# A strided convolution with its gradients on one core: 258-wide leaf planes, one transfer to turn both row parities, rows stored by parity

## The chip, the cores and the metric

The kernel runs on one core of a Trainium2 chip. The metric is device time in microseconds (us), from launch to end. Each number of the trace comes from one profiled execution; the time that counts is the median of several runs. The engines are TensorE (PE: matmuls; PEld: its weight loads), VectorE (DVE), ScalarE (ACT), GpSimd (POOL) and SyncE (SP). SP computes nothing here: it issues DMAs, one after the other, and a DMA that has to wait for its data holds back all that stand behind it in SP's queue.

## The reference

The forward pass is a convolution along time of 31 taps and stride 2, a normalisation of each channel over time, and a GELU. The outputs are the forward result and the gradients of all four inputs.

```python
B, T, D, K = 2, 16000, 256, 31          # x: (2, 16000, 256), w: (31, 256, 256), bf16
L = (T - K) // 2 + 1                    # 7985
h = sum over i of einsum('blc,cd->bld', x[:, i:i + 2 * L:2, :], w[i])
mu, var = mean and variance of h over l, for each image and channel
h = (h - mu) / sqrt(var + 1e-5) * gn_gamma + gn_beta
out = gelu(h, tanh form)
out_0 = out;  out_1 .. out_4 = vjp(grad_out): dx, dw, dgamma, dbeta
```

## The kernel before

The three convolutions (forward, gradient of x, gradient of w) are computed by a fast-FIR scheme with three branches A, B, C on each of several levels, so that fewer matmuls are needed and the operands are sums and differences of rows. The program has five stages. F0 and F1 are the forward pass of image 0 and image 1; beside F1, the element-wise work of image 0 (`gelu_unit`, 8 units) is done. G0 and G1 are the gradient of x (`input_grad`), in 8 chunks (4 of each image) of 2 halves and 3 branches; beside the first chunks the 8 gelu units of image 1 run. W is the gradient of w (`weight_grad`), in 9 combinations.

In G, a chunk's error rows are loaded with `e_load` (two DMAs, `dyd` and `hd`, for each half of the channels), made ready by `e_comp` (line 1201, 1203 or 1208, 1210, 1212, 1221) and spread into planes with channels on the partitions: a plane holds 256 rows and 2 or so from the chunk before, once for the even and once for the odd rows (index `j`). `g_sums` makes the sums of planes (line 1272). Matmuls (line 1317) read them as weights. `g_three_b` copies a PSUM bank with ACT (line 1344), `g_seed` combines banks with DVE (line 1384), `g_evac` takes results out of PSUM with ACT (`keep`, line 826) into `HO`, a single buffer, which a DMA stores to `out_1`; ACT writes it again only when that store has landed.

W needs the same planes with rows on the partitions. So `dl_turn` turns them by DMA: for each chunk nine leaves (3 branches by 3), each into one of four tiles `DNO`, and stores the tile to DRAM (`dl_d`). A leaf takes four turns, for two halves of the channels and two parities of the row, of 128 partitions by 256 columns (65,536 bytes) each, and one store of 262,144 bytes, in which the even and the odd row of a pair lie together in 1,024 bytes. That makes 8 x 9 x 4 = 288 turns and 72 stores. `d_tile` loads 19 rows a partition of one leaf in W. In F1, `gelu_unit` of image 0 turns its output by the same helper, in pieces of 128 partitions by 1,024 columns (262,144 bytes), two a unit.

Within a gelu unit of image 1, ACT's sigmoid (line 1098) writes the tile that the unit before has stored to `dyd`: it waits until that store has landed.

All DMAs of more than 4,096 bytes are issued by SP. Their place in its queue, and the order on each other engine, comes from a planner (`Plan`): each step is recorded with a duration, a DMA time, what it reads and writes; steps get a due time from the matmuls that they feed, moved by two tables (`lead` for a kind of step, `fine` for a kind in a chunk); a list scheduler then places them by due time. For a turn, the planner reckons 0.15 + 0.00105 us for each 256 bytes of SP's time, which for 65,536 bytes is 0.42 us.

Of the kernel before, what the change touches and what calls it, by code (L numbers as in the profile page):

```python
# [11 lines left out]
BF16 = mybir.dt.bfloat16  # L12
# [8 lines left out]
A, B_, C_ = 0, 1, 2  # L21
# [17 lines left out]
class Plan:  # L39
# [3 lines left out]
    def __init__(self, tc):  # L43
# [10 lines left out]
            "F0 f_evac last": -10.0,  # L54
            "F0 f_mm f_outer": -6.5,
            "F0 f_mm f_three_ac": -8.5,
            "F0 f_mm f_three_b": 10.5,
            "F0 f_outer forward": -67.5,
            "F0 f_seed forward": -35.5,
            "F0 f_three_b forward": -18.0,  # L60
            "F0 load f_evac": 11.5,
            "F0 put x_first": 36.5,
            "F0 tt f_sums": -48.5,
            "F0 tt third": -1.5,
            "F0 turn x_load": 16.5,
            "F0 ve f_seed": 9.0,
            "F0 ve_neg f_seed": 7.0,
            "F1 f_evac last": -45.0,
            "F1 f_mm f_leaf": -25.5,
            "F1 f_mm f_outer": 1.5,  # L70
            "F1 f_mm f_three_ac": 0.5,
            "F1 f_mm f_three_b": -23.0,
            "F1 f_outer forward": -10.0,
            "F1 f_seed forward": 15.0,
            "F1 f_three_b forward": -5.0,
            "F1 gelu_batch conv_stem_kernel": -39.0,
            "F1 gelu_unit gelu_batch": 4.0,
            "F1 keep f_evac": 3.0,
            "F1 load f_evac": 33.0,
            "F1 load gelu_unit": -2.0,  # L80
            "F1 tiny elem_finalize": 7.0,
            "F1 tiny fwd_stats": -1.5,
            "F1 tt f_sums": -18.5,
            "F1 tt gelu_unit": -25.0,
            "F1 turn gelu_unit": -11.0,
            "F1 turn x_load": 43.0,
            "F1 ve f_seed": 3.5,
            "F1 ve_neg f_seed": 7.5,
            "F1 w_sub f_again": 31.0,
            "F1 zero f_evac": 13.0,  # L90
            "F1 zero gelu_batch": 45.0,
            "G0 e_comp e_load": -0.5,
            "G0 g_mm g_three_b": -5.5,
            "G0 g_three_b input_grad": 6.5,
            "G0 gelu_unit gelu_batch": -1.0,
            "G0 keep g_evac": -4.5,
            "G0 keep g_seed": 6.0,
            "G0 load dl_turn": 9.5,
            "G0 load e_load": 15.0,
            "G0 load gelu_unit": 2.0,  # L100
            "G0 load load_w2": -18.0,
            "G0 plus g_seed": 5.0,
            "G0 tiny elem_finalize": -9.5,
            "G0 tt first": -60.0,
            "G0 tt gelu_unit": -0.5,
            "G0 tt second": 1.0,
            "G0 turn dl_turn": 1.0,
            "G0 turn gelu_batch": -8.5,
            "G0 zero e_comp": 7.5,
            "G1 e_comp e_load": 13.0,  # L110
            "G1 g_mm g_leaf": -1.0,
            "G1 g_mm g_outer": -6.0,
            "G1 g_mm g_three_ac": -8.0,
# [48 lines left out]
            "F0 turn x_load": {2: -23.0, 3: -23.0},
            "F0 ve f_first": {0: -19.0},
            "F0 ve f_seed": {0: 13.0, 1: -3.0, 2: 8.0, 3: -11.5},
            "F0 ve_neg f_seed": {0: 15.5, 3: 32.0},
            "F1 f_evac last": {2: -18.0, 3: 8.5},
            "F1 f_mm f_leaf": {3: -44.5},
            "F1 f_mm f_outer": {3: -4.5},
            "F1 f_mm f_three_ac": {0: 3.5, 1: 6.5, 2: 4.0, 3: -1.5},
            "F1 f_mm f_three_b": {0: 29.0, 1: 16.5, 3: -34.5},  # L170
            "F1 f_outer forward": {3: 3.5},
            "F1 f_seed forward": {3: -3.0},
            "F1 f_three_b forward": {0: 8.0, 1: 5.0, 3: -27.0},
            "F1 gelu_unit gelu_batch": {0: 1.0, 2: -8.5, 3: -15.5, 5: -13.5, 7: -16.0},
            "F1 keep f_evac": {3: 1.0},
            "F1 load f_evac": {3: -7.5},
            "F1 load gelu_unit": {6: 14.5, 7: -36.5},
            "F1 load out0_store": {1: 13.5, 4: 18.5, 7: 11.5},
            "F1 tiny elem_finalize": {0: -3.0},
            "F1 tiny fwd_stats": {0: -5.5},  # L180
            "F1 tt gelu_unit": {0: -56.0, 1: 30.0, 2: 23.5, 3: 6.0, 6: 6.5, 7: 9.5},
            "F1 tt second": {1: -3.5, 3: -65.0},
            "F1 tt third": {1: -29.5, 2: -5.5, 3: 5.5},
            "F1 turn gelu_batch": {0: -15.5, 1: 3.5, 2: 3.5, 3: 5.0, 4: -5.0, 5: 26.5},
            "F1 turn gelu_unit": {3: -38.5, 5: 17.5},
            "F1 turn x_load": {1: -9.5, 2: -41.0},
            "F1 ve f_seed": {2: -24.0, 3: -10.5},
            "F1 ve_neg f_seed": {2: 27.0, 3: -1.0},
            "F1 w_sub f_again": {3: -23.5},
            "F1 zero f_evac": {3: -11.0},  # L190
            "F1 zero gelu_batch": {7: -35.0},
            "G0 e_comp e_load": {0: -16.5, 1: -4.5, 2: -7.0, 3: 2.5},
            "G0 g_mm g_three_ac": {0: 0.5},
            "G0 g_mm g_three_b": {0: -2.5, 1: -3.5, 2: -2.5},
            "G0 g_three_b input_grad": {0: -1.0, 3: 2.0},
            "G0 gelu_unit gelu_batch": {0: 2.5, 1: -4.0, 2: 0.5, 3: 1.0, 6: -1.0},
# [260 lines left out]
def conv_stem_kernel(  # L457
# [16 lines left out]
    P = 128  # L474
# [3 lines left out]
    HM = 256  # L478
    XM = 272
    F = 4 * XM  # L480
    EM = 260
    plan = Plan(tc)
    add = plan.add

# [1370 lines left out]
```

## Time and profile before

| | us |
|---|---|
| median of 3 runs | 1333.9 (1332.7 to 1338.96) |
| the profiled execution | 1334.03 |
| its span, first to last instruction | 1332.3 |
| PE busy | 1163.7 (87%) |
| DVE busy | 983.5 (74%) |
| ACT busy | 568.3 (43%) |

Busy times are sums over the whole span, and the stages have different limits. F takes about the first 416 us of the span, G from there to about 1000 us, W the rest. DMA-issuing instructions are not counted as busy, so SP has no busy time on the page; it appears as "SPq" in the chain of waits and in the timeline, where a row of SP is the time that it spent on issuing that DMA. PEclk is the granted TensorE clock in parts of full speed. "L1317" is line 1317 of the kernel before.

### The profile page before, as it was taken

How to read it: one execution, taken by the hardware profiler on the slowest of the kernel's cores; microseconds unless marked ns; L12 is line 12 of the kernel's file. 1: busy time of each engine (PE TensorE's matmuls, PEld its weight loads, DVE VectorE, ACT ScalarE, POOL GpSimd, SP SyncE). 2: the span in 40 equal slices, each digit the busy share in tenths (PEclk: the TensorE clock that was granted, in tenths of full speed). 3: DMA queues.
4: the chain of work that ended last, by engine and by line, in shares of the span. 5: the costliest groups of instructions: out<-in, count | busy, mean ns of one | idle time of the engine just before them, and what ended most of it. 6: DMA issues, size and time to landing. Idle time of an engine off the chain costs nothing.

```text
span 1332.3 us, 18807 instructions
## 1 busy us (share of the span) xinstructions
PE 1163.7 (87%) x7646; PEld 760.9 (57%) x7700; DVE 983.5 (74%) x856; ACT 568.3 (43%) x849; POOL 22.8 (2%) x79
## 2 busy tenths in 40 slices
PE   6999999999999957578646888987887999899998
PEld 4888998777787423233212333433336866664785
DVE  8978778998998766476534547665648989678996
ACT  1445447778657755666422434642231221211100
POOL 0000000000000000001000000000000000000000
PEclk9999999999999979889977889988998999999999
DMA  7655688799657568775546445445379572799566
GB/s 189 125 122 168 124 167 208 144 202 219 170 170 277 169 189 237 189 201 155 133 109 205 132 117 157 122 133 184 105 224 302 195 264 77 212 318 329 197 223 153
DMA packets 360610, 243.61 MB, mean 183 GB/s; under 512 B 236572, under 2 KB 338684, under 8 KB 354044
## 3 DMA queue, kind: packets, MB, share of 16 engines
q1 hardware_dynamic: 360332, 242.41, 65.8%
q8 instruction: 60, 0.98, 0.3%
q14 instruction: 26, 0.21, 0.1%
q0 software_dynamic: 192, 0.00, 0.0%
HBM read 106.24 MB, written 80.30 MB: 140 GB/s over the span
## 4 chain that ended last, share of the span: by engine, by line
PE 27%; SPq 17%; DMA 9%; DVE 5%; ACT 3%; issue 3%; POOL 0%; DVEq 0%; ACTq 0%
PE ps L1549 20%; SPq L542 14%; PE ps L1317 7%; SPq L537 3%; DMA arena<-dyd 2%; DMA arena<-in_x_dram 2%; DVE arena L1272 1%; DMA out_dram<-arena 1%; ACT arena L826 1%; DMA arena<-dld 1%; DVE arena L1623 1%; DVE arena L1518 1%; DMA yd<-arena 1%; DMA arena<-arena 1%; DMA arena<-hd 1%
## 5 line engine op out<-in xcount | busy, mean ns | idle before, releaser
L1317 PE MATMUL ps<-arena 128*128 128x512 bf16 (+1 forms) x1880 | 445.8, 396 | 133.2 <-ACT arena L826 45.0
L731 PE MATMUL ps<-arena 128*128 128x256 bf16 (+4 forms) x3460 | 406.1, 281 | 12.7 <-DVE arena L673 5.5
L1317 PEld LDWEIGHTS <-arena 128*128 128x128 bf16 x1920 | 195.2, 102 | 382.5 <-issue 182.6
L731 PEld LDWEIGHTS <-arena 128*128 128x128 bf16 x3460 | 337.7, 98 | 81.0 <-DVE arena L673 5.8
L1549 PE MATMUL ps<-arena 128*128 128x256 bf16 (+1 forms) x2306 | 312.7, 298 | 18.8 <-DMA arena<-dld 9.4
L1549 PEld LDWEIGHTS <-arena 128*128 128x128 bf16 x2320 | 228.1, 98 | 103.7 <-issue 18.4
L826 ACT ACTIVATE arena<-ps 128x1024 f32<-128x1024 f32 (+1 forms) x143 | 144.5, 1019 | 311.7 <-PE ps L1549 99.3
L689 DVE TENSOR_TENSOR arena<-arena 128x2064 bf16<-128x2064 bf16 (+7 forms) x126 | 156.9, 1267 | 22.3 <-PE ps L731 21.6
L1272 DVE TENSOR_TENSOR arena<-arena 128x1032 bf16<-128x1032 bf16 (+2 forms) x120 | 84.5, 730 | 56.5 <-PE ps L1317 40.9
L1106 DVE TENSOR_TENSOR arena<-arena 128x2048 bf16<-128x2048 bf16 (+1 forms) x80 | 95.7, 1196 | 38.5 <-ACT arena L1098 33.0
L1384 DVE TENSOR_TENSOR ps<-ps,arena 128x2048 f32<-128x2048 f32 x40 | 91.7, 2296 | 36.9 <-PE ps L1317 25.9
L1518 DVE TENSOR_TENSOR arena<-arena 128x4096 bf16<-128x4096 bf16 x38 | 86.0, 2286 | 9.5 <-DMA arena<-in_x_dram 7.8
L1096 DVE SCALAR_TENSOR_TENSOR arena<-arena 128x2048 bf16<-128x2048 bf16 (+1 forms) x16 | 35.8, 2240 | 38.1 <-ACT arena L1093 37.8
L846 ACT ACTIVATE arena<-ps 128x512 bf16<-128x512 f32 (+1 forms) x64 | 37.1, 580 | 56.1 <-PE ps L731 55.1
L1091 ACT ACTIVATE arena<-arena,stats 128x1024 bf16<-128x1024 bf16 (+1 forms) x32 | 37.5, 1211 | 40.1 <-issue 14.8
L1639 ACT COPY ps<-ps 128x256 f32<-128x256 f32 x54 | 19.3, 357 | 81.5 <-PE ps L1549 80.4
L1221 ACT COPY arena<-arena 128x768 bf16<-128x768 bf16 (+1 forms) x64 | 36.0, 615 | 42.3 <-DVE arena L1212 42.1
L1614 DVE TENSOR_TENSOR arena<-arena 128x4096 bf16<-128x4096 bf16 x19 | 43.3, 2288 | 12.5 <-DMA arena<-in_x_dram 12.2
L1623 DVE TENSOR_TENSOR arena<-arena 128x2048 bf16<-128x2048 bf16 x38 | 46.3, 1222 | 7.8 <-PE ps L1549 7.0
L1384 DVE TENSOR_TENSOR arena<-ps,arena 128x2048 f32<-128x2048 f32 x16 | 36.6, 2290 | 20.3 <-ACT arena L826 14.8
L1697 DVE TENSOR_TENSOR arena<-arena 128x4608 bf16<-128x4608 bf16 x18 | 45.7, 2551 | 1.3 <-DMA arena<-dld 1.3
L801 ACT ACTIVATE arena<-ps 128x512 f32<-128x512 f32 x56 | 29.4, 603 | 36.8 <-PE ps L731 20.4
(78 smaller groups left out, 623.8 us busy)
## 6 DMA issues: line engine op xcount, KB each, us to landing
arena<-in_x_dram SPq DMA_DIRECT2D x40, 1024.0 KB, 8.3
arena<-dld SPq DMA_DIRECT2D x18, 1216.0 KB, 12.0
dld<-arena SPq DMA_DIRECT2D x72, 256.0 KB, 2.5
arena<-hd SPq DMA_DIRECT2D x32, 512.0 KB, 5.0
out_dram<-arena SPq DMA_DIRECT2D x14, 1024.0 KB, 5.3
vl<-arena SPq DMA_DIRECT2D x36, 256.0 KB, 2.7
arena<-vl SPq DMA_DIRECT2D x9, 1024.0 KB, 11.3
hd<-arena SPq DMA_DIRECT2D x8, 1024.0 KB, 6.2
```

The lines of the kernel that those rows point to most:

```text
L542: lambda: nc.sync.dma_start_transpose(out=out, in_=in_), dma=np_ * PK[256] / 16e3 * 1.03, ns=PK[256], tp=SH[256], slack=slack)
L689: lambda: nc.vector.tensor_tensor(out=o, in0=a, in1=b, op=ALU.add))
L731: yield nc.tensor.matmul(ps[:, dh, cs], lhsT=wt, rhs=mv, start=s0, stop=False, skip_group_check=True)
L826: lambda: nc.scalar.activation(out=out, in_=ps, func=ACT.Copy, scale=scale))
L1106: add("DVE", dve(nf), [o], [a, b_], lambda: V.tensor_tensor(out=o, in0=a, in1=b_, op=op))
L1272: lambda: nc.vector.tensor_tensor(out=o, in0=a, in1=b, op=ALU.subtract))
L1317: yield nc.tensor.matmul(ps[:, e, 0:wide], lhsT=lt, rhs=mv, start=s0, stop=False, skip_group_check=True)
L1384: lambda: nc.vector.tensor_tensor(out=o, in0=a, in1=b, op=ALU.add))
L1518: add("DVE", dve(4096), [o], [a, b], lambda: nc.vector.tensor_tensor(out=o, in0=a, in1=b, op=ALU.add))
L1549: yield nc.tensor.matmul(ps[:, s, c0:c1], lhsT=lt, rhs=mv, start=s0, stop=False, skip_group_check=True)
L1623: add("DVE", dve(2048), [o], [u, v], lambda o=o, u=u, v=v: nc.vector.tensor_tensor(out=o, in0=u, in1=v, op=ALU.subtract))
L1697: add("DVE", dve(4608), [o], [u, v], lambda: nc.vector.tensor_tensor(out=o, in0=u, in1=v, op=ALU.subtract))
```

## The change

The planes are 258 instead of 260 elements wide, so that the 258 of the even rows and the 258 of the odd rows lie with no gap between them. One turn now takes columns 2 to 513 of the two together: rows 2 to 257 of the first parity and rows 0 to 255 of the second, 128 partitions by 512 columns (131,072 bytes). A leaf takes two turns. The tile is kept as two blocks, one for each parity, and stored by two DMAs of 131,072 bytes, in pieces of 512 bytes, into a DRAM tensor that has the two parities apart. `d_tile` loads 10 rows of one block and 9 of the other with a DMA each; W's indices into that tile change with it. The rows of zeros ahead of and behind the data are four small stores a leaf instead of two. The planner's time for a turn is at least 1.24 us, and the two tables have new values throughout (one line of each is shown).

```diff
-            "F0 f_mm f_outer": -6.5,
+            "F0 f_mm f_outer": -14.0,
...
-            "G0 keep g_evac": {0: 3.0, 1: -0.5},
...
-    EM = 260
+    EM = 258
...
-    NDL = 2112
-    dl_d = [[dram.tile([NDL, D], BF16, name=f"dld{b}_{i}") for i in range(9)] for b in range(NB)]
+    dl_d = [[dram.tile([2, 1056, D], BF16, name=f"dld{b}_{i}") for i in range(9)] for b in range(NB)]
...
     def turn(out, in_, nbytes, slack=None):
         np_ = nbytes / 256
-        add("SP", 0.15 + 0.00105 * np_, [out], [in_],
+        add("SP", max(1.24, 0.15 + 0.00105 * np_), [out], [in_],
...
-                pl = planes(br, lf)
+                pl = leaf(br, lf)
                 for dh in range(2):
-                    for j in range(2):
-                        turn(o[:, :, j, dh * P:(dh + 1) * P], pl[j][:, dh, 0:256], 65536)
-                t = dl_d[b][3 * MIR[br] + MIR[lf]][:]
-                dst = bass.AP(tensor=t.tensor, offset=t.offset + ((48 if b else 0) + 512 * c) * D,
-                              ap=[[2 * D, P], [256 * D, 2], [1, 2 * D]])
-                load(dst, o.rearrange("p m j d -> p m (j d)"), 262144, 1024, "POOL")
+                    turn(o.rearrange("p j m d -> p (j m) d")[:, :, dh * P:(dh + 1) * P],
+                         pl[:, dh].rearrange("p j f -> p (j f)")[:, 2:514], 131072)
+                for j in range(2):
+                    r0 = 24 * b + 256 * c + 2 * (1 - j)
+                    load(dl_d[b][3 * MIR[br] + MIR[lf]][j, r0:r0 + 256, :].rearrange("(m p) d -> p m d", p=P), o[:, j], 131072, 512,
+                         "POOL")
...
+        def leaf(br, lf):
+            return pair(br)[1] if lf == B_ else GL[br][:, 0 if lf == A else 1]
+
         def planes(br, lf):
-            v = pair(br)[1] if lf == B_ else GL[br][:, 0 if lf == A else 1]
-            return [v[:, :, j] for j in range(2)]
+            return [leaf(br, lf)[:, :, j] for j in range(2)]
...
-        t = dl_d[b][3 * i1 + i2][:]
-        load(D2_[n > 0][b].rearrange("p r d -> p (r d)"),
-             bass.AP(tensor=t.tensor, offset=t.offset, ap=[[16 * D, P], [1, 19 * D]]), 19 * 65536, 4096)
+        for j, (r, k) in enumerate(((0, 10), (10, 9))):
+            t = dl_d[b][3 * i1 + i2][j]
+            load(D2_[n > 0][b][:, r:r + k].rearrange("p r d -> p (r d)"),
+                 bass.AP(tensor=t.tensor, offset=t.offset, ap=[[8 * D, P], [1, k * D]]), k * 65536, 4096)
...
-                u, v = (both(D2[0][:, k], D2[1][:, k], [[2 * D, 9], [1, D]]) for k in (o_, 1))
+                u, v = (both(D2[0][:, k], D2[1][:, k], [[D, 9], [1, D]]) for k in (o_, 10))
...
-                load(dl_d[0][i][2048:2064, :], zt2[0:16], 8192, 512, "POOL", slack=300.0)
-                load(dl_d[1][i][0:48, :], zt2[0:48], 24576, 512, "POOL", slack=300.0)
+                for t, r0, r1 in ((dl_d[0][i][0], 0, 2), (dl_d[0][i][1], 1024, 1026), (dl_d[1][i][0], 0, 26), (dl_d[1][i][1], 0, 24)):
+                    load(t[r0:r1, :], zt2[0:r1 - r0], 512 * (r1 - r0), 512, "SP", slack=300.0)
...
-        zero(ET[i].rearrange("p d k j f -> p (d k j) f")[:, :, 257:EM], 48)
-        zero(GS[i][:, 1, :, 1, :, 257:EM], 12)
+        zero(ET[i][:, :, 3, 1, 257:EM], 2)
```

Three places of SP's queue show what moves. In the rows, `dld0_3` is the leaf tensor 3 of image 0, `dyd1_0` and `hd1_0` are chunk 0 of image 1, the last number is a buffer's; line 537 (550 after) issues a plain DMA and line 542 (555 after) a turn.

The first place is the start of G0, from the store `yd0` of the second gelu unit of image 1 to its store `dyd1_0`. Before:

```order
L537 DMA yd0_76<-arena_118 128x2x1024
L542 DMA_TRANSPOSE arena_118<-arena_118 128x2x128 x7
L537 DMA arena_118<-dyd0_2_70 128x2048
L542 DMA_TRANSPOSE arena_118<-arena_118 128x2x128 x4
L537 DMA arena_118<-hd0_2_62 128x2048
L537 DMA dyd1_0_72<-arena_118 256x1x1024
```

After:

```order
L550 DMA yd0_76<-arena_118 128x2x1024
L550 DMA dld0_8_88<-arena_118 128x2x256
L555 DMA_TRANSPOSE arena_118<-arena_118 128x4x128 x2
L555 DMA_TRANSPOSE arena_118<-in_grad_out_dram 128x8x256
L550 DMA dyd1_0_72<-arena_118 256x1x1024
```

Eleven turns and two loads stood between the two stores; two wider turns, one turn of the incoming gradient (which stood behind them) and a store of a leaf stand there now.

The second place is G0's end, from two leaf stores to the load of the second half of `hd1_0`, the first chunk of image 1. Before:

```order
L537 DMA dld0_0_80<-arena_118 128x2x512
L537 DMA dld0_2_82<-arena_118 128x2x512
L542 DMA_TRANSPOSE arena_118<-arena_118 128x2x128 x11
L537 DMA dld0_8_88<-arena_118 128x2x512
L542 DMA_TRANSPOSE arena_118<-arena_118 128x2x128
L537 DMA dld0_6_86<-arena_118 128x2x512
L542 DMA_TRANSPOSE arena_118<-arena_118 128x2x128
L537 DMA arena_118<-hd1_0_64 128x2048
```

After:

```order
L555 DMA_TRANSPOSE arena_118<-arena_118 128x4x128
L550 DMA dld0_7_87<-arena_118 128x2x256 x2
L550 DMA dld0_0_80<-arena_118 128x2x256 x2
L550 DMA dld0_1_81<-arena_118 128x2x256 x2
L550 DMA dld0_5_85<-arena_118 128x2x256 x2
L555 DMA_TRANSPOSE arena_118<-arena_118 128x4x128
L550 DMA dld0_2_82<-arena_118 128x2x256 x2
L550 DMA arena_118<-hd1_0_64 128x2048
```

Thirteen turns stood in the last rows ahead of that load; two stand there now, and ten stores of half a leaf.

The third place is in G1, between the eleventh and the twelfth store to `out_1`. Before:

```order
L537 DMA out_1_dram<-arena_118 128x4096
L542 DMA_TRANSPOSE arena_118<-arena_118 128x2x128 x9
L537 DMA dld1_7_96<-arena_118 128x2x512
L537 DMA dld1_8_97<-arena_118 128x2x512
L537 DMA dld1_4_93<-arena_118 128x2x512
L542 DMA_TRANSPOSE arena_118<-arena_118 128x2x128 x10
L537 DMA dld1_6_95<-arena_118 128x2x512
L542 DMA_TRANSPOSE arena_118<-arena_118 128x2x128 x2
L537 DMA out_1_dram<-arena_118 128x4096
```

After:

```order
L550 DMA out_1_dram<-arena_118 128x4096
L555 DMA_TRANSPOSE arena_118<-arena_118 128x4x128 x2
L550 DMA dld1_4_93<-arena_118 128x2x256 x2
L555 DMA_TRANSPOSE arena_118<-arena_118 128x4x128 x3
L550 DMA dld1_3_92<-arena_118 128x2x256 x2
L550 DMA dld1_5_94<-arena_118 128x2x256 x2
L550 DMA out_1_dram<-arena_118 128x4096
```

Twenty-one turns and four stores stood between the two; five turns and six half stores stand there now.

## Rows read from the trace of the kernel before

**Rows 1.** The page, part 4: the chain that ended last, by line.

```profile
PE ps L1549 20%; SPq L542 14%; PE ps L1317 7%; SPq L537 3%; DMA arena<-dyd 2%; DMA arena<-in_x_dram 2%; DVE arena L1272 1%; DMA out_dram<-arena 1%; ACT arena L826 1%; DMA arena<-dld 1%; DVE arena L1623 1%; DVE arena L1518 1%; DMA yd<-arena 1%; DMA arena<-arena 1%; DMA arena<-hd 1%
```

**Rows 2.** Windows: stretch, length, busy (count) by engine, PEclk, DMA share, GB/s.

```profile
0.00:416.00 416.00, 403.23 (x3432) 335.04 (x3434) 361.92 (x352) 235.71 (x435) 8.50 (x31) 1.00 0.72 169
...
443.00:666.00 223.00, 160.94 (x679) 70.34 (x692) 141.07 (x144) 129.20 (x152) 8.47 (x22) 0.90 0.64 174
666.00:705.00 39.00, 14.69 (x58) 6.24 (x59) 13.73 (x30) 7.43 (x11) 0.11 (x1) 0.68 0.41 112
705.00:992.00 287.00, 242.42 (x1022) 106.09 (x1042) 159.96 (x130) 117.43 (x136) 5.16 (x24) 0.91 0.52 148
...
1007.00:1332.00 325.00, 312.00 (x2304) 227.56 (x2316) 276.12 (x170) 53.98 (x88) 0.53 (x1) 0.99 0.71 222
```

**Rows 3.** Lines 542 and 537, 440 to 992 us: count, ns min/median/max on SP.

```profile
L542 SPq DMA_TRANSPOSE arena<-arena x289: 1167/1244/4231, 444.0 to 978.1; - x145
...
L537 SPq DMA_DIRECT2D dld<-arena x72: 359/512/1930, 469.9 to 980.6; - x72
```

**Rows 4.** Timeline of SP: start us, us, engine, line, DMA, count.

```profile
233.01 2.63 SPq L542 DMA_TRANSPOSE arena<-arena  x2
...
534.16 14.21 SPq L542 DMA_TRANSPOSE arena<-arena  x11
```

**Rows 5.** Timeline of all engines, 479 to 508 us, with idle time ahead and releaser.

```profile
479.91 1.22 DVE L1106 TENSOR_TENSOR arena<-arena 128x2048 bf16<-128x2048 bf16 x1
...
483.83 8.99 SPq L542 DMA_TRANSPOSE arena<-arena  x7
...
499.25 0.57 SPq L537 DMA_DIRECT2D dyd<-arena  x1
...
504.44 1.91 ACT L1098 ACTIVATE arena<-arena 128x2048 bf16<-128x2048 bf16 x1 [6.53 <-DMA dyd<-arena]
...
506.89 1.44 PE L1317 MATMUL ps<-arena 128*128 128x512 bf16 x3 [5.72 <-ACT ps L1344]
```

**Rows 6.** Waits, 443 to 666 us: in total, times, longest.

```profile
PE ps L1317 <- ACT ps L1344: 42.4, 12, 9.9
```

**Rows 7.** Timeline of all engines, 672 to 706 us.

```profile
673.13 1.23 DVE L1212 TENSOR_TENSOR arena<-arena 128x2048 bf16<-128x2048 bf16 x1
...
697.54 0.57 SPq L537 DMA_DIRECT2D arena<-hd  x1
...
701.48 0.81 DVE L1201 TENSOR_SCALAR arena<-arena,stats 128x2048 bf16<-128x2048 bf16 x1 [19.78 <-DMA arena<-hd]
...
704.56 1.01 PE L1317 MATMUL ps<-arena 128*128 128x256 bf16 x3 [23.11 <-DVE ps L1384]
```

**Rows 8.** Waits, 705 to 992 us.

```profile
ACT arena L826 <- DMA out_dram<-arena: 38.9, 4, 14.2
PE ps L1317 <- ACT arena L826: 34.7, 11, 7.5
```

**Rows 9.** Timeline of PE, 836 us on: a stretch with no wait.

```profile
836.78 24.98 PE L1317 MATMUL ps<-arena 128*128 128x512 bf16 x112 [0.22 <-issue]
```

**Rows 10.** DMA queues and issues: count, KB each, median us to landing.

```profile
q1 hardware_dynamic: 360332, 242.41, 65.8%
...
arena<-dld SPq DMA_DIRECT2D x18, 1216.0 KB, 12.0
dld<-arena SPq DMA_DIRECT2D x72, 256.0 KB, 2.5
...
arena<-arena SPq DMA_TRANSPOSE x305, 2.4
...
out_dram<-arena SPq DMA_DIRECT2D x30, 128.0 KB, 2.0
```

**Rows 11.** Tile dld, SP's issues of zeros: count, ns min/median/max.

```profile
L537 SPq DMA_DIRECT2D dld<-zt x18: 414/423/1521, 113.6 to 125.5; - x18
```

**Rows 12.** Line 1272, all of its instructions: ns min/median/max, forms.

```profile
L1272 DVE TENSOR_TENSOR arena<-arena x120: 683/693/1240, 416.5 to 945.6; 128x1032 bf16<-128x1032 bf16 x80, 128x1036 bf16<-128x1036 bf16 x32, 128x2072 bf16<-128x2072 bf16 x8
```

More of the change, by code (lines that the diff above doesn't have):

```diff
@@ L93, in __init__ @@
-            "G0 g_mm g_three_b": -5.5,
+            "F0 f_evac last": -9.0,
+            "F0 f_mm f_leaf": -119.5,
+            "F0 f_mm f_outer": -14.0,
+            "F0 f_mm f_three_ac": -8.0,
+            "F0 f_mm f_three_b": 32.5,
+            "F0 f_mm pe_turn": -75.5,
+            "F0 f_outer forward": -106.0,
+            "F0 f_seed forward": -12.0,
+            "F0 f_three_b forward": -26.5,
+            "F0 keep f_evac": -48.0,
+            "F0 load f_evac": 33.0,
+            "F0 load put": 9.5,
@@ new lines, in __init__ @@
+            "F0 load x_load": 13.5,
+            "F0 tt f_sums": -72.0,
+            "F0 tt third": 4.5,
+            "F0 turn w2_part": -15.5,
+            "F0 turn x_load": 24.0,
+            "F0 ve f_first": -78.0,
+            "F0 ve_neg f_seed": 20.5,
+            "F0 w_sub f_first": 12.0,
+            "F0 w_sum w2_part": 26.0,
+            "F0 zero f_evac": -11.0,
+            "F1 f_evac last": -30.0,
+            "F1 f_mm f_leaf": -44.0,
+            "F1 f_mm f_outer": -28.0,
+            "F1 f_mm f_three_ac": 0.5,
@@ new lines, in __init__ @@
+            "F1 f_mm f_three_b": -5.5,
+            "F1 f_outer forward": -3.0,
+            "F1 f_seed forward": 11.5,
+            "F1 f_three_b forward": 4.0,
+            "F1 gelu_unit gelu_batch": -1.0,
+            "F1 keep f_evac": 15.5,
+            "F1 load gelu_unit": 30.0,
+            "F1 tiny elem_finalize": -71.5,
+            "F1 tt f_sums": -53.0,
+            "F1 tt gelu_unit": -16.5,
+            "F1 tt second": -25.5,
+            "F1 tt third": -8.0,
+            "F1 turn gelu_unit": -8.0,
@@ new lines, in __init__ @@
+            "F1 load gelu_unit": {0: -17.0, 2: -9.5, 4: 31.0, 5: -40.5},
+            "F1 load out0_store": {7: 37.0},
+            "F1 tt f_sums": {0: 2.0},
+            "F1 tt gelu_unit": {0: 3.5, 6: -46.0},
+            "F1 tt third": {1: 27.5, 3: -11.5},
+            "F1 turn gelu_batch": {0: -35.5},
+            "F1 turn gelu_unit": {0: 58.0, 6: 25.0},
+            "F1 turn x_load": {1: 21.0, 2: 15.0, 3: -71.5},
+            "F1 ve f_seed": {3: 24.5},
+            "F1 ve_neg f_seed": {3: 2.0},
@@ new lines, in __init__ @@
+            "G1 g_mm g_three_ac": {1: -8.0, 2: -6.0},
+            "G1 g_mm g_three_b": {0: 9.0, 2: -2.0},
+            "G1 keep g_evac": {2: 3.0, 3: 1.0},
+            "G1 load dl_turn": {0: -3.5, 1: -1.5},
+            "G1 load e_load": {1: -2.0, 2: -0.5, 3: -0.5},
+            "G1 load g_evac": {2: 4.0, 3: -2.5},
+            "G1 plus g_seed": {0: 2.0, 1: 0.5, 3: 0.5},
+            "G1 spread e_comp": {2: 2.0},
+            "G1 tt first": {0: 18.0},
+            "G1 tt second": {0: -26.0, 1: -13.0},
@@ L1439, in input_grad @@
                 plan.part = c
-                first, second, third, planes = g_sums(t)
+                first, second, third, planes, leaf = g_sums(t)
                 for pr in range(2):
```

297 lines of the change are left out of this document (126 added, 171 removed), and 4 rows, old and new, of the table MIR.

## The prediction

> **What bounds the kernel now.** I read the page's chain first, then windows by stage, then SP's queue in the slow stage, and last what PE waits for there. The chain has PE's own lines, as expected of a tuned kernel, and beside them 14% on line 542, the issuing of turns [rows 1]. The windows say where: in F (to 416 us) PE is busy 403.2 of 416 and in W 312.0 of 325, both at a granted clock of 0.99 to 1.00; in G, from 443 to 992 us, it is busy 160.9 + 14.7 + 242.4 = 418 of 549 us, and the clock is at 0.68 to 0.91 [rows 2]. So F and W have nothing to give, and G has. What the matmuls of G need follows from a stretch without a wait: 112 in 24.98 us, 0.223 us each, and there was still a little in it; I take 0.22 [rows 9]. The 679 + 58 + 1022 = 1759 records of G then need 387 us. The excess is 549 - 387 = 162 us: 131 of idle PE and 31 of slower clock.
>
> SP's queue is full there. A turn takes 1.244 us in the median [rows 3], 14.21 / 11 = 1.29 with the gap behind it [rows 4]; 289 of them make 373 us. The 72 stores of leaves, 0.51 [rows 3] and, as an estimate, 0.1 of gap, make 44. These alone are 417 of the 549 us, and the loads and stores of the error rows, of `out_1` and of the gelu units come on top, in the same order. Three places show what this does to PE.
>
> At 481.1 us the last multiplication of a gelu unit is done and its tile may go out; SP issues that store at 499.25, with turns ahead of it. ACT's sigmoid waits for it until 504.44, the copy of line 1344 stands behind that sigmoid, and PE starts 5.72 us late [rows 5]. In this stretch PE waits 42.4 us in all for line 1344 [rows 6], of 62 idle. At 674.4 DVE has freed the buffer of `hd1_0`'s second half; the load is issued at 697.54, 23 us later, DVE waits 19.78 for it and PE 23.11 [rows 7]. In the last stretch ACT waits 38.9 us for stores to `out_1`, in four waits, and PE 34.7 for ACT [rows 8].
>
> **The change part by part.** Turns: 288 become 144. The cost of one of 512 columns isn't in the trace; it lies between one of 256 columns, 1.29 with its gap, and the turns of F1, of 1,024 columns, which take 2.63 / 2 = 1.32 [rows 4]. I take 1.29. Twice that would be 2.58, which only a cost by columns could give, and the 1,024 columns exclude it as far as the trace goes. So SP loses 144 x 1.29 = 186 us.
>
> Stores of leaves: 72 more at 0.61 add 44 us to SP. At the least they take 0.36 and a gap (33), at the most the 1.93 of the slowest (146, only when the queue is full). Net, SP's work in G falls by 142 us; with the 373 + 44 before, turns and stores are then 275 instead of 417 of the 549 us. SP is no longer longer than PE's 387.
>
> What PE gains is less than its excess, since waits between PE, ACT and DVE stay, and a queue that is used for well over half of the time still holds things up. By stretch. From 443 to 666: 679 x 0.22 = 149 of 223, an excess of 74. Between the two stores of the first place shown in the change stood 11 turns (14.2 us) and 2 loads (1.2); now 2 turns (2.6), one turn of the gradient and a store. The 18 us that the store came late become about 8. That is 10 for one unit of eight, and most of what is waited for has this cause: I take 45, three fifths. From 666 to 705 the excess is 39 - 13 = 26, in one stall; ahead of the load of `hd1_0` the last 13 turns and 2 stores (18.0 us) become 2 turns and 10 stores (8.7), and the queue is not behind to begin with: I take 15. From 705 to 992: 1022 x 0.22 = 225 of 287, an excess of 62. Between the two stores to `out_1` 21 turns and 4 stores (29.5 us) become 5 turns and 6 stores (10.1); these late stores are behind about two thirds of PE's wait, some 23, and the clock that comes back with fuller matmuls is worth some 7 of this stretch's share: I take 30. Together 90. The bounds of this sum are nothing (another wait takes over everywhere) and 162.
>
> What is late next: in the first stretch the unit's own chain on ACT and DVE, busy 129 and 141 of 223 us; in the last the copy out of PSUM behind the last matmul of a bank.
>
> Tiles `DNO`: a tile is now filled by 2 turns (2.6), lands (2.4), goes out by two stores (1.2) and lands again (2.0 for 128 KB, 2.5 for 256 KB) [rows 10]: some 8.3 us instead of 5.2 + 2.4 + 0.6 + 2.5 = 10.7. With four tiles that is one leaf in 2.1 us, less than SP's 3.8 a leaf. No wait comes from there.
>
> Smaller edits. 258 instead of 260: line 1272's forms of 1,036 and 1,032 both take 0.69 us [rows 12], so two columns fewer give nothing; should the odd pitch cost half of DVE's speed, 120 x 0.7 = 84 us would fall on an engine that is idle 234 us of the three stretches [rows 2]; below nothing there is no reason for a gain. Zeros: 18 more stores of 0.42 and a gap [rows 11], 9 us of SP in F0, beside matmuls that have their operands; at worst some 9 us. Loads of W: 18 more issues at about 0.5, 9 us of SP over 325; PE is busy 96% there, and the pieces together bring the same bytes. The first ones stand between G and W: one issue more is 0.5 us late, an earlier end of the turns brings as much; from -4 to +4. The memsets of the pads are POOL's, which is idle. The new order of F and W: -5 to +5, since PE has 13 us idle in each. All at 0.
>
> Sum: 1334.03 - 90 = 1244 us. The profiled execution is 0.13 us from the median of 1333.9, so nothing is to be corrected.
>
> **A rule that speaks against it.** The trace has 2.0 us to landing for a store of 128 KB and 2.5 for 256 KB [rows 10], so a halved transfer is nearly as long. The Trainium skill, "DMA: Bandwidth & Descriptors", section "Rules for kernel authors", asks for many small transfers to be joined into a large one, with 1 MiB and more for the best rate; the change does the reverse with stores and loads of leaves. Were each of the 90 more to cost its 2.0 us [rows 10] one after another, the 180 us would eat the whole gain; the trace agrees only that a half is no half in latency. Its milder case, in which the DMA engines bind, is rival 3.
>
> **Rivals.** 1: the wait changes hands. SP is relieved, but PE then waits for ACT and DVE at the same banks. For it: PE's waits are put down to ACT and DVE, not to DMA. Against: at each of the three places they wait for a DMA themselves. Then only the stall before 705 and a part of the stores to `out_1` go: 15 + 20 = 35, 1299 us.
>
> 2: all waits of G have SP behind them, and the clock returns to 1.0. Then up to 140 of the 162 go: 1194 us. Against: the queue stays the one way for everything.
>
> 3: the DMA engines take over. 360,332 packets took 65.8% of 16 engines' 1332 us, 38.9 ns each [rows 10]. 72 x 256 = 18,432 packets more are 18,432 x 38.9 / 16 = 45 us. In G the engines were busy for 0.64 x 223 + 0.41 x 39 + 0.52 x 287 = 308 of 549 us [rows 2]; 353 of 459 would be 0.77. If they bound it, 45 of the 90 go again: 1289. Against: F ran at 0.72 with PE full.
>
> 4, the other side: a turn's time on SP goes by its columns. Then 144 turns take as long as 288, and 44 us of stores are added to a queue that is full: from 1334, if gaps in it take them all, to 1378; I say 1360. It decides from 373 + 44 - 88 = 329 us for 144, that is 2.3 us a turn, on. Against: the turns of F1.
>
> **How the numbers follow.** Forecast 0.70, rival 1 0.13, rival 2 0.06, rival 3 0.05, rival 4 0.06. With each of the three terms a third off, all one way, the forecast's own range is 1214 to 1274; toward rivals 1 and 3 I go up to 1303, toward rival 2 down to 1198. A change of 0.5%, 6.7 us, is about what a measurement of this kernel can tell from none. Faster: forecast, rivals 2 and 3, and most of rival 1: 0.90. Slower: rival 4: 0.06. Same: 0.04.
>
> **What would show it.** Turns of 512 columns at about 1.25 us each on SP, 144 of them; line 542's share of the chain at half or less; from G's first matmul to its last about 90 us less, of it half before the end of the gelu units; PE's wait for line 1344 below 20 us, ACT's for `out_1` below 15; the load of `hd1_0`'s second half within 10 us of its buffer; the granted clock in G nearer to 1. F and W keep their lengths to within 5 us each. I am wrong if turns take over 2 us, if PE's idle time in G stays over 100 us with SP idle beside it, or if F or W grow by more than 10.

## The result, and the profile after

The changed kernel takes 1215.0 us (median of four runs, 1212.4 to 1218.2) beside 1333.5 for the kernel before (four runs, 1332.7 to 1339.0). The ratio is 0.9105, with a 95% interval of 0.9071 to 0.9138. The forecast was 1244 with a range of 1198 to 1303: right in sign and range, and 29 us short of the gain. The profiled execution took 1214.1 us with a span of 1212.4; before it was 1332.3, so 119.9 us are to be placed.

The chain that ended last, by line, is this in the page of the changed kernel (line 555 issues turns and line 550 plain DMAs; 1565, 1332 and 744 are the matmuls of W, G and F):

```profile
PE ps L1565 17%; PE ps L1332 13%; DMA arena<-in_x_dram 3%; DMA arena<-dld 3%; DVE arena L1533 2%; SPq L550 2%; DVE ps L1399 1%; DVE arena L1630 1%; DMA arena<-arena 1%; SPq L555 1%; DVE arena L1639 1%; ACT arena L839 1%; DMA dld<-arena 1%; DMA arena<-hd 1%; DVE arena L1713 1%
```

The 14% of turns [rows 1] are 1% now. The windows of the changed kernel follow, with the columns of [rows 2] and cut at the same events, as near as they go: F, the gelu units, the change of stage after them, the rest of G, W.

```profile
0.00:416.00 416.00, 403.02 (x3404) 333.82 (x3406) 360.31 (x350) 234.74 (x431) 7.91 (x28) 0.99 0.74 174
443.00:611.00 168.00, 156.91 (x712) 71.27 (x724) 142.34 (x146) 134.85 (x155) 8.95 (x22) 0.99 0.88 231
611.00:640.00 29.00, 22.84 (x106) 10.44 (x106) 17.40 (x29) 10.78 (x14) 0.44 (x1) 0.98 0.88 209
640.00:865.00 225.00, 214.73 (x971) 97.42 (x989) 156.65 (x126) 114.05 (x131) 6.05 (x20) 0.99 0.70 186
882.00:1212.00 330.00, 314.13 (x2303) 229.14 (x2316) 275.61 (x170) 53.88 (x88) 0.53 (x1) 0.98 0.69 213
```

The reader is to see three things beside [rows 2]. PE is busy for 394 of 422 us in G, where it was 418 of 549. The granted clock there is 0.98 to 0.99 instead of 0.68 to 0.91, so nearly all of it is at the upper of the two levels, 2.4 GHz. And F is as before while W is not shorter, but 5 us longer.

The groups of PE tell the same by stage: the busy time, the mean of one, and the idle time before the matmuls of a line, in the page of the changed kernel:

```profile
L1332 PE MATMUL ps<-arena 128*128 128x512 bf16 (+1 forms) x1880 | 416.3, 379 | 28.5 <-DVE ps L1399 7.2
L744 PE MATMUL ps<-arena 128*128 128x256 bf16 (+4 forms) x3460 | 408.4, 282 | 12.9 <-DMA arena<-in_x_dram 5.8
L1565 PE MATMUL ps<-arena 128*128 128x256 bf16 (+1 forms) x2305 | 314.8, 299 | 28.4 <-DVE arena L1630 24.9
```

and in the kernel before:

```profile
L1317 PE MATMUL ps<-arena 128*128 128x512 bf16 (+1 forms) x1880 | 445.8, 396 | 133.2 <-ACT arena L826 45.0 <-ACT ps L1344 44.4 <-DVE ps L1384 38.8
L1549 PE MATMUL ps<-arena 128*128 128x256 bf16 (+1 forms) x2306 | 312.7, 298 | 18.8 <-DMA arena<-dld 9.4 <-DVE arena L1623 6.4 <-DVE arena L1614 1.6
```

G loses 104.7 us of idle PE and 29.5 of busy time. The 29.5 are the clock. The same count of matmuls stands in both groups, but of those of 128x512 the trace of before has 134 that ran wholly at the lower level, 1.2 GHz, at 631 ns in the median, and this one has 17; at the upper level they take 379 ns, and 117 fewer at 0.252 us each are 29.5. From PE's own instructions, in us:

| stretch | before | after | difference |
|---|---|---|---|
| to G's first matmul | 414.5 | 414.5 | 0 |
| G, first matmul to the end of the last | 582.4 | 451.0 | -131.4 |
| PE idle between G and W | 9.4 | 15.8 | +6.4 |
| W, first matmul to the end | 326.0 | 331.1 | +5.1 |
| sum | 1332.3 | 1212.4 | -119.9 |

Now SP, whose queue the prediction was about. Its two groups in G, 440 to 866 us, in the changed kernel (count, ns min/median/max):

```profile
L555 SPq DMA_TRANSPOSE arena<-arena x144: 1188/1267/3040, 438.7 to 849.6; - x144
...
L550 SPq DMA_DIRECT2D dld<-arena x144: 367/493/2031, 449.6 to 854.0; - x144
```

A turn of 512 columns takes 1.267 us in the median, one of 256 took 1.244 [rows 3]. Since long ones count too, the issues are also summed one by one from the trace, each with the short gap behind it (some 0.045 us) but without SP's waits for data, which a merged row of the timeline can hold. Before, from 440 to 993 us, 289 turns took 393.5 us (mean 1.36), the 72 stores of leaves 43.5, and all of SP's issues 522 of 553, or 94%. In the changed kernel, 440 to 866 us, 144 turns take 206.9 us (mean 1.44), 144 stores 88.4 (mean 0.61), and everything together 357 of 426, or 84%. Turns and stores fell from 437 to 295.

The three places: at the first, the last multiplication of the gelu unit ends at 477.3 us, the store of `dyd1_0` goes out 5.9 us later instead of 18, and the sigmoid (line 1111 now) has no wait in front of it. The timeline of all engines:

```profile
480.70 2.46 SPq L555 DMA_TRANSPOSE arena<-in_grad_out_dram  x1
483.20 0.60 SPq L550 DMA_DIRECT2D dyd<-arena  x1
...
490.78 1.90 ACT L1111 ACTIVATE arena<-arena 128x2048 bf16<-128x2048 bf16 x1
```

At the second, DVE frees the buffer at 618.72 + 1.22 = 619.9, the load of `hd1_0`'s second half is issued 6.6 us later instead of 23, and PE's stop there is 5.34 instead of the 23.11 of [rows 7], and behind another releaser:

```profile
618.72 1.22 DVE L1225 TENSOR_TENSOR arena<-arena 128x2048 bf16<-128x2048 bf16 x1
...
626.55 0.44 SPq L550 DMA_DIRECT2D arena<-hd  x1
...
630.66 0.81 DVE L1214 TENSOR_SCALAR arena<-arena,stats 128x2048 bf16<-128x2048 bf16 x1 [5.82 <-DMA arena<-hd]
...
639.46 3.75 PE L1332 MATMUL ps<-arena 128*128 128x512 bf16 x10 [5.34 <-ACT ps L839]
```

For the third, the waits of all of G, 416 to 866 us (total, times, longest):

```profile
PE ps L1332 <- DVE ps L1399: 7.2, 7, 3.0
ACT arena L839 <- DMA out_dram<-arena: 7.1, 2, 5.6
PE ps L1332 <- ACT ps L839: 6.7, 2, 5.3
PE ps L1332 <- ACT ps L1359: 6.5, 6, 2.3
PE ps L1332 <- ACT arena L839: 5.7, 8, 2.5
```

PE's wait for the copy (line 1359 now) was 42.4 us in the gelu units alone [rows 6] and is 6.5 in all of G; ACT's for the stores to `out_1` was 38.9 in the last stretch [rows 8] and is 7.1. What remains is 28 us in many short pieces.

What got longer is the crossing from G to W, here in the timeline of all engines:

```profile
862.15 0.55 SPq L550 DMA_DIRECT2D arena<-in_x_dram  x1
...
874.41 2.29 DVE L1630 TENSOR_TENSOR arena<-arena 128x4096 bf16<-128x4096 bf16 x1 [10.41 <-DMA arena<-in_x_dram]
...
881.28 2.96 PE L1565 MATMUL ps<-arena 128*128 128x256 bf16 x13 [15.81 <-DVE arena L1630]
```

W's first sum (line 1630) needs a piece of `x` that is issued 3 us before G's last matmul ends and lands 12 us later. The chain that ended last shows what held that issue:

```profile
853.96 8.14 DMA dld<-arena
...
862.15 12.14 DMA arena<-in_x_dram
```

SP could issue the load of `x` only when the last store of a leaf had landed, 8.14 us after its issue. Before, PE waited 9.4 at the crossing, for a leaf.

### The profile page after: what moved, and what is told of

Same layout as the page of the kernel before. It is cut to its first block, busy times and chain, and to the rows that moved or that the text cites. A ratio compares the mean times of both kernels' runs of the same rounds, so it can differ in the third digit from the quotient of the medians.

```text
span 1212.4 us, 18743 instructions
## 1 busy us (share of the span) xinstructions
PE 1138.9 (94%) x7645; PEld 757.9 (63%) x7700; DVE 982.9 (81%) x856; ACT 569.1 (47%) x849; POOL 27.2 (2%) x77
## 3 DMA queue, kind: packets, MB, share of 16 engines
q1 hardware_dynamic: 377783, 242.35, 74.4%
## 4 chain that ended last, share of the span: by engine, by line
PE 31%; DMA 8%; DVE 7%; SPq 3%; issue 1%; ACT 1%; DVEq 0%; POOL 0%
PE ps L1565 17%; PE ps L1332 13%; DMA arena<-in_x_dram 3%; DMA arena<-dld 3%; DVE arena L1533 2%; SPq L550 2%; DVE ps L1399 1%; DVE arena L1630 1%; DMA arena<-arena 1%; SPq L555 1%; DVE arena L1639 1%; ACT arena L839 1%; DMA dld<-arena 1%; DMA arena<-hd 1%; DVE arena L1713 1%
## 5 line engine op out<-in xcount | busy, mean ns | idle before, releaser
L1332 PE MATMUL ps<-arena 128*128 128x512 bf16 (+1 forms) x1880 | 416.3, 379 | 28.5 <-DVE ps L1399 7.2
L744 PE MATMUL ps<-arena 128*128 128x256 bf16 (+4 forms) x3460 | 408.4, 282 | 12.9 <-DMA arena<-in_x_dram 5.8
L1565 PE MATMUL ps<-arena 128*128 128x256 bf16 (+1 forms) x2305 | 314.8, 299 | 28.4 <-DVE arena L1630 24.9
L702 DVE TENSOR_TENSOR arena<-arena 128x2080 bf16<-128x2080 bf16 (+7 forms) x126 | 156.2, 1264 | 32.3 <-PE ps L744 26.2
L1285 DVE TENSOR_TENSOR arena<-arena 128x1032 bf16<-128x1032 bf16 (+1 forms) x120 | 84.4, 726 | 28.6 <-PE ps L1332 23.2
L780 ACT ACTIVATE ps<-ps 128x256 f32<-128x256 f32 x75 | 27.8, 371 | 40.0 <-PE ps L744 38.7
L1234 ACT COPY arena<-arena 128x768 bf16<-128x768 bf16 (+1 forms) x64 | 36.5, 616 | 19.2 <-DVE arena L1225 15.8
L814 ACT ACTIVATE arena<-ps 128x512 f32<-128x512 f32 x56 | 29.5, 601 | 25.1 <-PE ps L744 19.7
```

The source lines that it names most:

```text
L702: lambda: nc.vector.tensor_tensor(out=o, in0=a, in1=b, op=ALU.add))
L744: yield nc.tensor.matmul(ps[:, dh, cs], lhsT=wt, rhs=mv, start=s0, stop=False, skip_group_check=True)
L1285: lambda: nc.vector.tensor_tensor(out=o, in0=a, in1=b, op=ALU.subtract))
L1332: yield nc.tensor.matmul(ps[:, e, 0:wide], lhsT=lt, rhs=mv, start=s0, stop=False, skip_group_check=True)
L1565: yield nc.tensor.matmul(ps[:, s, c0:c1], lhsT=lt, rhs=mv, start=s0, stop=False, skip_group_check=True)
```

## The experiments

Theory: the time went with SP's issue time, most of it with the turns. Rivals: the new order (tables and planner) did it, or another effect of the wider layout, or the DMA engines. Each experiment's time is the median of its runs, each ratio is to the kernel before on the same chip.

**e1_split: the layout, the stores and the order of the change, but every wide turn issued as two.** The planner still sees one turn; its issue is a pair.

```diff
-                    turn(o.rearrange("p j m d -> p (j m) d")[:, :, dh * P:(dh + 1) * P],
-                         pl[:, dh].rearrange("p j f -> p (j f)")[:, 2:514], 131072)
+                    ot = o.rearrange("p j m d -> p (j m) d")[:, :, dh * P:(dh + 1) * P]
+                    it = pl[:, dh].rearrange("p j f -> p (j f)")[:, 2:514]
...
+                        for k in range(2):
+                            yield nc.sync.dma_start_transpose(out=ot[:, 2 * k:2 * k + 2], in_=it[:, 256 * k:256 * k + 256])
```

> The changed kernel with its order, layout and stores; only each turn of 512 columns is issued as two of 256 columns, one behind the other in the same place (288 turns instead of 144). Theory 1 (the gain is SP's issue time of the turns): 144 x 1.29 = 186 us come back to a queue that issues for about 361 us in the 426 us of G; 547 us no longer fit, G lasts 530 us or more, and the time is 1310 to 1345 us. Theory 2 (the gain is the new order by the two tables and the planner's cost of a turn): most of the gain stays, below 1260 us. Theory 3 (the gain is the two parities stored apart, with the new loads in W): no change, 1215 us.

Measured: 1369.0 us, ratio 1.0271 (1.0244 to 1.0298): 154 us above the changed kernel, and 36 above the kernel before. Its turns on SP:

```profile
L1279 SPq DMA_TRANSPOSE arena<-arena x288: 1167/1244/3186, 439.9 to 1006.9; - x144
```

PE in its G (line 1341):

```profile
L1341 PE MATMUL ps<-arena 128*128 128x512 bf16 (+1 forms) x1920 | 447.0, 396 | 136.4 <-ACT arena L839 82.6 <-DVE ps L1408 28.2 <-ACT ps L839 17.0
```

ACT's wait for stores to `out_1` in its G:

```profile
ACT arena L839 <- DMA out_dram<-arena: 54.8, 6, 19.4
```

G is 590 us again, with idle time and matmul means as before the change. SP is occupied 525 of 560 us from 440 on, 94%. Theories 2 and 3 are out; theory 1 has the direction, and the time lies 24 us beyond its range. Of the 154 us, 16 are idle PE between G and W, 32.1 us instead of 15.8. So the layout and the order, with 72 more stores but without the saved turns, are worth less than nothing. The order was planned for 144 turns, though: the 154 us are what the turns cost in this order, and e7_oldplan below splits the gain another way. The 38.9 ns a packet of [rows 10] make 11 us of the 4,608 packets that this kernel has more (382,391 against 377,783), and the DMA share of its G is 0.57 beside 0.79 in the changed kernel; DMA engines can't explain the 154.

**e2_split0 and e3_split1: the same pairs in one image alone.** The edit is that of e1_split, under the condition `b == 0` or `b == 1`.

> The changed kernel, same order; only the leaves of image 0 (chunks 0 to 3, turned in G0 and the start of G1) are turned by twice as many turns of 256 columns, 72 turns or 93 us of SP more. All turns split cost 154 us. Theory A (the gain came in the shares of the forecast, 60 of 90 up to the end of the stall behind the gelu units): about 100 us come back, 1300 to 1325 us. Theory B (each part of G gained what its queue was over): SP has some 35 us free in that part, so 93 - 35 = 58 us come back, 1265 to 1290 us.

> The changed kernel, same order; only the leaves of image 1 (the rest of G) are turned by twice as many turns of 256 columns, 72 turns or 93 us of SP more. Theory A (shares of the forecast, 30 of 90 behind the stall): about 50 us come back, 1255 to 1275 us. Theory B: SP has some 30 us free there, 63 us come back, and more where the last turns hold up the loads of W, as they do with all turns split: 1275 to 1310 us.

Measured: 1298.9 (0.9747, 0.9715 to 0.9779) and 1283.7 (0.9633, 0.9598 to 0.9668), so +84 for image 0 and +69 for image 1: 152 together, beside the 154 of both at once. PE in G of e2_split0:

```profile
L1341 PE MATMUL ps<-arena 128*128 128x512 bf16 (+1 forms) x1920 | 441.4, 393 | 91.2 <-ACT arena L839 37.9 <-DVE ps L1408 28.7 <-ACT ps L839 15.7
```

and of e3_split1:

```profile
L1341 PE MATMUL ps<-arena 128*128 128x512 bf16 (+1 forms) x1920 | 428.9, 385 | 70.0 <-ACT arena L839 50.1 <-ACT ps L839 8.2 <-DVE ps L1408 5.8
```

The first lies 1 us below theory A's range and 9 above theory B's, so it fits neither; the second lies in theory B's. The effects add, so there is no single place that decides. A turn more costs 84 / 72 = 1.16 us in image 0 and 69 / 72 = 0.95 in image 1, a little less than what it occupies SP, 1.24. Of the 69 us, 17 are idle PE between G and W (32.4 us instead of 15.8), as theory B expected of the last turns.

**e8_stores: the changed kernel, with each store of half a leaf issued as two of a quarter.** No turn is touched, and the same bytes go, in 380,087 packets of that queue instead of 377,783.

```diff
+                    def halves(dst=dst, src=o[:, j]):
+                        for m in range(2):
+                            yield nc.sync.dma_start(out=dst[:, m], in_=src[:, m])
+                    plan.ops[-1]["fn"] = halves
```

> The changed kernel, same order; only each of the 144 stores of leaves is issued as two of 65,536 bytes (288 stores), some 0.6 us of SP each, 86 us more. Theory 1 (SP's issue time is what counts, of whatever kind of DMA): 86 - 65 free = 21 us at the least come back, up to 70: 1236 to 1285 us. Rival (it was the turns as such, their way through the DMA engines): under 5 us, 1210 to 1220 us.

Measured: 1262.3 us, 0.9473 (0.9418 to 0.9527), or +47. Its stores on SP:

```profile
L1280 SPq DMA_DIRECT2D dld<-arena x288: 319/432/2162, 452.8 to 909.1; - x144
```

PE in its G:

```profile
L1337 PE MATMUL ps<-arena 128*128 128x512 bf16 (+1 forms) x1920 | 434.2, 388 | 54.7 <-ACT arena L839 20.8 <-ACT ps L839 15.1 <-DVE ps L1404 11.2
```

The time lies in the range of theory 1 and far from the rival's. The summed stores take 159 us of SP instead of 88; 70 us more on SP cost 47. So it isn't the turn as such: plain stores on that queue cost too, 0.67 us here for each that they occupy it longer. Across these kernels G's length goes along with SP's sum from 440 us on: 522 and 582 us before, 525 and 590 in e1_split, 425 and 495 here, 357 and 451 in the changed kernel.

**e4_replan: the kernel before, with the planner's new cost of a turn alone.** The order tables stay as they were.

```diff
-        add("SP", 0.15 + 0.00105 * np_, [out], [in_],
+        add("SP", max(1.24, 0.15 + 0.00105 * np_), [out], [in_],
```

> The kernel before, with one edit: the planner reckons at least 1.24 us for a turn. Transfers and tables are those of before. Theory 1: the queue has the same 288 turns and 72 stores and is full in G however it is ordered, so 1320 to 1350 us. Theory 2: the right cost alone puts urgent loads and stores ahead, below 1300 us.

Measured: 1361.8 us, 1.0217 (1.0189 to 1.0245): slower by 29, and above the ranges of both theories. PE by stage (G, F, W):

```profile
L1317 PE MATMUL ps<-arena 128*128 128x512 bf16 (+1 forms) x1920 | 445.6, 394 | 110.7 <-ACT arena L826 62.1 <-DVE arena L1272 16.1 <-DVE ps L1384 15.7
L731 PE MATMUL ps<-arena 128*128 128x256 bf16 (+4 forms) x3460 | 412.0, 283 | 27.2 <-DVE arena L673 12.1 <-DVE small L1159 6.7 <-DMA arena<-in_x_dram 5.6
L1549 PE MATMUL ps<-arena 128*128 128x256 bf16 (+1 forms) x2320 | 315.3, 299 | 44.5 <-DMA arena<-dld 37.0 <-DVE arena L1623 3.1 <-DVE arena L1614 1.3
```

With the right cost PE idles 23 us less in G, but 14.5 more in F and 25.7 more in W. In this kernel a truer cost in one place wasn't an improvement; that the tables had been found with the false one is the likely reason, and no run shows it.

**e5_oldtab: the changed kernel with the tables of the kernel before**, so with the new transfers and the planner's new cost (of 346 changed lines, four):

```diff
-            "F0 f_evac last": -9.0,
-            "F0 f_mm f_leaf": -119.5,
...
+            "F0 f_evac last": -10.0,
+            "F0 f_mm f_outer": -6.5,
...
```

**e7_oldplan: e5_oldtab with the planner's old cost as well**, so the transfers alone:

```diff
-        add("SP", max(1.24, 0.15 + 0.00105 * np_), [out], [in_],
+        add("SP", 0.15 + 0.00105 * np_, [out], [in_],
```

> The changed kernel with both tables of numbers taken from the kernel before; transfers, layout and the planner's cost of a turn are the changed ones. Theory 1: the relieved queue keeps most of the gain, at most 1255 us; the tables are worth 0 to 40 us. Theory 2: without the new tables little of the gain is left, above 1290 us.

> The changed kernel with both tables and the planner's cost of a turn (0.69 us for 512 columns) from the kernel before: the transfers alone. Theory 1 (the tables fit the planner that they were searched with): F and W lose less than with old tables and the new cost (25 and 47 us of idle PE there), so 1235 to 1260 us. Theory 2 (the new cost is worth something by itself, as the queue's head is known better): slower than with it, above 1280 us.

Measured: 1270.9 (0.9536, 0.9518 to 0.9554) and 1270.7 (0.9535, 0.9502 to 0.9568): equal in sum, though not by stage (idle PE is 25.3 and 15.8 us in F, 47.2 and 56.3 in W and ahead of it). Each time lies between the ranges of its two theories. So the transfers alone bring 62 us, the tables 56 more, which is above the 0 to 40 expected of them, and the planner's cost beside the old tables nothing. PE in G and W of e7_oldplan:

```profile
L1318 PE MATMUL ps<-arena 128*128 128x512 bf16 (+1 forms) x1920 | 425.0, 382 | 41.8 <-DVE ps L1385 16.0 <-ACT arena L825 12.6 <-ACT ps L1345 12.3
...
L1551 PE MATMUL ps<-arena 128*128 128x256 bf16 (+1 forms) x2320 | 318.7, 300 | 56.3 <-DMA arena<-dld 20.1 <-DVE arena L1616 18.0 <-DVE arena L1625 8.4
```

and PE's two largest waits in its W:

```profile
PE ps L1551 <- DMA arena<-dld: 20.1, 3, 18.9
PE ps L1551 <- DVE arena L1616: 18.0, 2, 16.5
```

The transfers alone already shorten G from 582 to 473 us, by 109. Of that, 47 are lost again, most of it in W and ahead of it: idle PE there goes from 18.8 to 56.3. Its longest wait, 18.9 us at 1112, is for loads of leaves that SP issues behind eight loads of `x`. The halved loads are not needed for it: e4_replan, which loads whole leaves, stops as long at the same place of W. In e7_oldplan and in e4_replan:

```profile
1112.06 1.01 PE L1551 MATMUL ps<-arena 128*128 128x256 bf16 x4 [18.94 <-DMA arena<-dld]
...
1209.54 1.01 PE L1549 MATMUL ps<-arena 128*128 128x256 bf16 x4 [20.27 <-DMA arena<-dld]
```

What the two have in common is the old tables beside something else that was changed. The new tables take W's idle back to 28.4, shorten G by a further 22 us, and bring F's from 15.8 to 12.9.

**e6_poolstore: the changed kernel with the stores of leaves issued by POOL**, which is nearly idle otherwise (27 us busy), in an order planned anew for it.

```diff
-    def load(out, in_, nbytes, run, eng="SP", slack=None):
-        if plan.stage in ONE and nbytes > 4096:
+    def load(out, in_, nbytes, run, eng="SP", slack=None, keep_eng=False):
+        if plan.stage in ONE and nbytes > 4096 and not keep_eng:
...
-                         "POOL")
+                         "POOL", keep_eng=True)
```

> The changed kernel with the 144 stores of leaves issued by POOL instead of SP, and the order planned for it. SP loses another 144 x 0.6 = 86 us in G. Theory 1a (after the change SP no longer bounds anything): within 0.5%, 1209 to 1221 us. Theory 1b (SP still holds things up, as a queue in use for 85% of G does): PE's remaining idle time of 28 us in G shrinks, 1190 to 1208 us. A price to watch for: POOL's copies of the rows from the chunk before stand behind stores that wait for turns; if these decide, slower than 1221 us.

Measured: 1224.4 us, 0.9193 (0.9172 to 0.9215): 9 us slower than the changed kernel, and 3 above the upper end of theory 1a. Its stores on POOL:

```profile
L550 POOL DMA_DIRECT2D dld<-arena x144: 723/723/806, 443.9 to 853.1; - x144
```

Its turns on SP, 440 to 866 us:

```profile
L555 SPq DMA_TRANSPOSE arena<-arena x145: 1189/1267/3785, 438.8 to 848.9; - x145
```

PE in its G:

```profile
L1332 PE MATMUL ps<-arena 128*128 128x512 bf16 (+1 forms) x1920 | 419.0, 379 | 24.2 <-DVE ps L1399 12.1 <-ACT ps L1359 5.9 <-ACT ps L839 3.2
```

G is 448.9 us beside 451: nothing that can be told from none. Yet SP was relieved: the 88 us of stores went, the turns took 221 us instead of 207 (mean 1.53 instead of 1.44) and all other issues 72 instead of 62, so SP's sum fell from 357 to 294 us, 69% of the stretch. Taking another 63 us from SP brought G nothing, where 70 us more had cost 47 in e8_stores. So, as far as this run shows, SP's issue time no longer bounds G in the changed kernel; theory 1b is out. PE is busy for 94% of G here, so there was little left to win. One reservation stays, since the order is planned anew and POOL has work that it had not: a gain by the relief could be hidden by a loss from these. The profiled execution, 1219.5, is 5.4 us longer than that of the changed kernel, and it loses this outside G: PE idles 2.2 us more in F and 4.9 in W and ahead of it.

## Why the prediction was right, and where its size was off

**SP's sum.** Right to the microsecond, in part by luck. Turns: forecast -186, measured 206.9 - 393.5 = -187. Stores: forecast +44, measured 88.4 - 43.5 = +45. Net -142, as forecast. The prediction took 1.29 us for every turn; the means were 1.36 before and 1.44 after, since some issues are long, and 0.07 x 289 and 0.15 x 144 are both some 21 us and cancel. A turn's time goes by issue, not by columns, so rival 4 is out.

**What PE makes of it.** Here the size failed: the prediction gave G 90 of the 142 us that SP loses, and of PE's 162 us of excess; G gained 131. By terms:

- Gelu units, -45 forecast. From the first multiplication of a gelu unit to the end of all units it was 230.6 us and is 169.3: -61. "Three fifths" of the 74 was too little. Idle PE in this stretch went from 62.1 to 11.1, so nearly all of it went with SP's load. Ahead of that first multiplication G became 6 us longer (21.5 to 27.4).
- The stall at `hd1_0`, -15 forecast. PE's wait went from 23.1 to 5.3, -18, with the load 6.6 us behind its buffer.
- The rest of G, -30 forecast. From the units' end to G's last matmul there are 75.9 us less (330.3 to 254.4), some 58 of them without the stall. The prediction counted the late stores' 23 us and 7 of the clock. In its window PE's idle time fell from 44.6 us to 10.3, and the clock went from 0.91 to 0.99.
- The clock. The prediction named 31 us of excess from it and claimed 7 of the last stretch in the open; the matmuls of G got 29.5 back. In G the lower level stood for 119.5 us before and for 10.2 now.

So rival 2 ("all waits of G have SP behind them, and the clock returns") was nearer to the truth than its 0.06: of its 140, 131 came. Its time of 1194 was missed by 20 us, 9 of them in G and 11.5 in the crossing and W. Rival 1 is out: PE's remaining waits for ACT and DVE are short. Rival 3 is out as a bound: G's DMA share is 0.79, where the prediction worked out 0.77, and PE waits 28 us in all; in e1_split and e8_stores time comes back while the share falls, to 0.57 and 0.71.

**What was put at nothing.** The wait between G and W (-4 to +4) and W (-5 to +5) together measured +11.5. For W, 3.2 us of its 5.1 are idle PE and 2.1 busy; what causes them was not tried. The crossing's 6.4 come, by the chain, from the load of `x` behind the last leaf's store. In the sum: G 41 more than forecast, crossing and W 11.5 less, 29.9 in all, which is 1244 - 1214.1.

The new order stood in the sum with -5 to +5, for F and W alone, and all of G's 90 us were put down to the transfers. The runs split it otherwise: by the transfers alone (e7_oldplan) G is 109 us shorter and W 36 longer, and the time is 1270.7, 27 above the forecast; the tables then bring 56 us, 31 of them in W and 22 in G, and the time is 29 below it. So the missing term is the order's: the prediction did not ask what the old tables would make of the new transfers. That 1244 lies midway between the two times is luck. What in the new transfers the old tables don't fit stays open; it need not be the halved loads, since e4_replan has whole ones and W is 24 us longer there too.

The rest of what stood at nothing was so, with one remark: line 1272's sums (1285 now) take 0.689 us in the median at the new pitch [rows 12], F is 414.5 us with its doubled zeros, and no wait of PE, ACT or DVE in G is put down to a store of leaves. SP itself does wait for such stores to land before it turns into a tile `DNO` again, 12.5 us in G in six waits, where the prediction saw no wait at all.

**Signs.** Turns 1.25 (1.267 measured), line 542's share at half (1%), waits for line 1344 under 20 (6.5), ACT's for `out_1` under 15 (7.1), the load within 10 us (6.6), the clock near 1 (0.99): as forecast. G "about 90 shorter" and "F, W within 5 us" were missed, by 41 and by 0.1. Of G's gain 55 us, or 42%, came before the end of the gelu units, for the half that was forecast.

**The rule of the skill that was weighed**, to join small transfers (the Trainium skill, "DMA: Bandwidth & Descriptors", "Rules for kernel authors"): the change halves stores and loads, and G became 131 us shorter, so there the rule did not decide. But the change also joins turns, two into one, as the rule asks, and e1_split shows that the gain hangs on them. In e8_stores, where the halving of the stores goes once more, the rule's direction holds: +47 us, 0.33 for each issue added.

## What to carry to other kernels

Sum the issue times of one engine's DMA queue over a stage and set them beside the stage's length. Where the sum was 94% of it, waits that the profile puts down to ACT or DVE went back to that queue, and most of each microsecond saved on it came back (here 0.67 to 0.92 of one). At 84% that was over: in e6_poolstore 63 us more taken from SP brought G nothing. Where PE idles, look at its clock too: here 105 us less of idle came with 29.5 less of matmul time. And judge a planner's cost, or new transfers, together with the numbers of the order found under the old ones: the truer cost alone lost 29 us, and the new transfers under the old tables gave away 56 of the 118 us.

## What the runs showed of the hardware

- The time for which a turn occupies SP hardly depends on its width in this range: 1.244 us for 256 columns and 1.267 for 512 in the median, least 1.167 and 1.188.
- A plain store's issue is not free either: 0.49 us (median) for 128 KB and 0.43 for 64 KB on SP, and a very regular 0.723 on POOL.
- Some issues take much longer than the median: 26 of 144 turns over 1.4 us in the changed kernel, up to 3.04, and 50 of 145 in e6_poolstore, up to 3.79, at the same median of 1.267. What the long ones wait for stays open.
